# Steps of six score tiles, a fixed accumulator and a factored mixing in a gated-attention and token-mixing kernel

## The chip, the core and the metric

The kernel runs on one core of a Trainium2 chip. The core has five engines with a queue of instructions each: PE (TensorE, matrix products, whose results go to PSUM, eight banks of 512 fp32 columns on 128 partitions), DVE (VectorE), ACT (ScalarE), POOL (GpSimd) and SP, which only issues DMAs here. Each engine works through its queue in order; semaphores hold an instruction until what it reads is there and what it overwrites has been read. The metric is the device time of one execution in microseconds (us).

## The reference

Eight batches, each with a sequence of S = 3200 and a model width of D = 256. z is S x 64, u and v are S x D, and all inputs and the output are fp32.

```python
scores = (1 / S) * z @ z.T                    # S x S per batch
attn   = maximum(scores, 0) ** 2
x      = u * (attn @ v)                       # S x D
wq, wk = x @ w_q, x @ w_k                     # S x 64
W_tok  = (wq @ wk.T) / sqrt(64)               # S x S
out    = maximum(W_tok @ x, 0) @ w_out        # S x D
```

Nothing nonlinear stands between W_tok and x, so the kernel never forms W_tok. It uses W_tok @ x = x @ (w_q @ w_k.T @ G), with G = x.T @ x, a 256 x 256 matrix per batch, and moves all scale factors into one final factor.

## The kernel before, in words

The queries of a batch (columns of the scores) are cut into seven groups of 512, 512, 512, 512, 384, 384 and 384 columns. For each group the kernel goes through 25 tiles of 128 keys. A score tile is a matmul with 64 rows (z has 64 features); zT holds z transposed twice, in partitions 0 to 63 and 64 to 127, so that the two score matmuls of a pair use different halves of the PE array. A pair fills one PSUM tile of two banks (`scores`, L202).

The pair then goes through two stages. `first_stage` writes g = max(4 sc, 0) in fp32 to SBUF, on DVE (L226) or ACT (L222), and so empties PSUM. `second_stage` squares g to fp16, on ACT (L236) or POOL (L238). The result, at, is the stationary side of the second product with v (`outs`, L253), which adds up over the 25 tiles in a tile "acc" of two banks. `gate` multiplies acc by u (L273) and gives x. `turn_x` transposes x by a DMA from SP's queue (L281).

All PSUM tiles (score pairs, acc, and the products named below) take turns in one pool of four slots of two banks.

The work is a software pipeline of steps written out by hand. A step has four score tiles (GRP = 4), and the second product follows three steps later (LAG = 3). In a step, the order on every engine is: scores, first stages, what is due at the start of the step, second stages of the step before, the second product, what is due at the end of the step. `two` puts a product at the end of one step and its eviction at the start of the next.

When a batch's seven groups are done, `gram` makes G (L291), `mixw` multiplies it by M = w_k w_q^T, made once at the start by `weights_1` and `weights_2` (L309, a tile "jtp", in fp32), and then, one group of the following batch at a time, `mix` (L328, four matmuls of the group's width with 128 rows) and `proj` (L350, the product with w_out) make the output, which ACT scales (L387) and SP's queue stores (L388). The last batch's mixing stands at the end by itself, with DVE scaling (L383). xT of a group is thus read a whole batch after it is written.

z of the next batch is loaded in fp32 by SP's queue (L115), cast and transposed in 32 x 32 blocks by DVE in five pieces (`turn_z`, L123 and L124), put in place by eight DMAs (`spread_z`, L131) and doubled by one more (`double_z`, L141). v of the next batch is loaded and cast by a DMA from POOL's queue (`load_v`, L110). z of the first batch is cast and transposed in four pieces, on PE (`transpose_first`, L101).

## Time and profile before

| | |
|---|---|
| median of 3 runs | 953.89 us (953.76 to 954.2) |
| the profiled execution, own time | 955.04 us |
| its span, first to last instruction | 953.2 us |
| PE busy | 919.7 us, 7521 matmuls |
| DVE busy | 702.5 us |
| POOL busy | 611.6 us |
| ACT busy | 544.3 us |
| DMA moved | 92.51 MB, mean 97 GB/s |
| mean granted PE clock | 0.998 of full |

In the views below a line reads: line of the kernel, engine, operation, output <- inputs, shapes, count, then busy time or idle time and what ended it. In a timeline the first column is the start in us from the span's start and the second is how long the run of like instructions took. In a window's row each engine's busy time stands with its count, in the order PE, PEld (weight loads), DVE, ACT, POOL, and then the PE clock, the DMA share and GB/s. In the list of waits the three numbers are total us, times, longest us. A matmul's recorded end is modelled, so PE's busy time covers some short waits. For a DMA, "to landing" is the time from its issue to the last semaphore update.

### The profile page before, as it was taken

Reading aid. Unit: us, or ns where it says so; the run is one execution under the profiler, and the core shown is the slowest. Engines: PE = TensorE matmul, PEld = TensorE weight load, DVE = VectorE, ACT = ScalarE, POOL = GpSimd, SP = SyncE. Lnnn points to the kernel's source line nnn. Section 1 sums busy time; section 2 is a strip of 40 time slices with the busy share of each in tenths; the row PEclk is TensorE's granted clock in tenths of the full one; section 3 lists DMA queues with packets and bytes.
Section 4 is the critical chain, followed back from the end, with each engine's and each line's share of the span. In section 5 each row is a group of like instructions: output and inputs, shape, how many; then the busy total and the mean of one; then the engine's idle time right before and its main releaser. Section 6 shows DMA issues by size and latency. Waiting matters only on the chain.

```text
span 953.2 us, 18224 instructions
## 1 busy us (share of the span) xinstructions
PE 919.7 (96%) x7521; PEld 622.7 (65%) x7521; DVE 702.5 (74%) x760; ACT 544.3 (57%) x627; POOL 611.6 (64%) x375
## 2 busy tenths in 40 slices
PE   6999999999999999999999999999999999999996
PEld 3666676666766666666666667666676666766674
DVE  4988858778587776877678776877758877587753
ACT  4555545566456664566455664655646566466643
POOL 6877756767566764757566665666657666567650
PEclk9999999999999999999999999999999999999999
DMA  9942257432582346632566424843338433123224
GB/s 156 143 82 47 59 90 144 94 93 75 94 157 70 91 104 105 119 90 70 129 80 118 109 77 105 124 94 97 83 88 125 103 88 89 48 74 88 71 71 139
DMA packets 204707, 92.51 MB, mean 97 GB/s; under 512 B 127120, under 2 KB 204176, under 8 KB 204624
## 3 DMA queue, kind: packets, MB, share of 16 engines
q1 hardware_dynamic: 178576, 77.97, 34.2%
q0 software_dynamic: 25776, 13.11, 11.1%
q8 instruction: 59, 0.97, 0.4%
q10 hardware_dynamic: 272, 0.26, 0.1%
q14 instruction: 24, 0.20, 0.1%
HBM read 59.38 MB, written 26.21 MB: 90 GB/s over the span
## 4 chain that ended last, share of the span: by engine, by line
PE 83%; DVE 10%; issue 4%; ACT 2%; DMA 1%; DVEq 0%; ACTq 0%
PE acc L253 51%; PE sc L202 17%; DVE g L226 7%; PE fo L350 5%; PE xtx L291 5%; PE mx L328 4%; PE jtp L309 1%; DVE zs L123 1%; ACT rt L340 1%; DVE x_sb L273 1%; DMA out_dram<-fo 0%; PE ztp L101 0%; ACT g L222 0%; DMA z<-in_z_dram 0%; DVE wo L174 0%
## 5 line engine op out<-in xcount | busy, mean ns | idle before, releaser
L238 POOL TENSOR_TENSOR at<-g 128x1024 f16<-128x1024 f32 (+2 forms) x354 | 595.2, 1694 | 310.5 <-DVE g L226 282.1
L226 DVE TENSOR_SCALAR g<-sc 128x1024 f32<-128x1024 f32 (+2 forms) x562 | 595.2, 1096 | 212.3 <-PE sc L202 201.4
L253 PE MATMUL acc<-v_sb,at 128*128 128x256 f16 x5000 | 608.3, 274 | 0.4 <-DVE g L226 0.4
L253 PEld LDWEIGHTS <-at 128*128 128x128 f16 x5000 | 461.5, 98 | 169.1 <-issue 104.7
L236 ACT ACTIVATE at<-g 128x1024 f16<-128x1024 f32 (+2 forms) x354 | 327.2, 952 | 23.0 <-DVE g L226 21.5
L222 ACT ACTIVATE g<-sc 128x1024 f32<-128x1024 f32 (+2 forms) x146 | 132.8, 913 | 273.5 <-PE sc L202 267.1
L202 PE MATMUL sc<-zT 64*128 64x512 f16 (+1 forms) x1400 | 207.0, 361 | 15.2 <-DVE g L226 11.1
L202 PEld LDWEIGHTS <-zT 64*128 64x128 f16 x1400 | 47.5, 94 | 113.0 <-issue 108.7
L340 ACT ACTIVATE rt<-mx 128x1024 f16<-128x1024 f32 (+1 forms) x56 | 52.0, 931 | 40.1 <-PE mx L328 40.1
L273 DVE TENSOR_TENSOR x_sb<-acc,u_sb 128x512 f16<-128x512 f32 x112 | 65.4, 625 | 9.1 <-PE acc L253 8.8
L350 PE MATMUL fo<-wo,rt 128*128 128x256 f16 x400 | 53.0, 273 | 3.7 <-ACT rt L340 3.7
L387 ACT ACTIVATE fo<-fo 128x1024 f32<-128x1024 f32 (+1 forms) x49 | 45.6, 930 | 17.4 <-PE fo L350 17.4
L328 PE MATMUL mx<-xT_sb,jt 128*128 128x512 f16 (+1 forms) x224 | 52.2, 356 | 0.7 <-ACT jt L320 0.7
L350 PEld LDWEIGHTS <-rt 128*128 128x128 f16 x400 | 38.0, 98 | 12.8 <-ACT rt L340 7.8
L291 PE MATMUL xtx<-x_sb 128*128 128x256 f16 x400 | 45.0, 273 | 0.0
L291 PEld LDWEIGHTS <-x_sb 128*128 128x128 f16 x400 | 39.1, 98 | 4.5
L328 PEld LDWEIGHTS <-jt 128*128 128x128 f16 x224 | 21.6, 98 | 13.4 <-ACT jt L320 1.1
L123 DVE CAST zs<-z 128x320 f16<-128x320 f32 x35 | 24.3, 696 | 0.0
L302 ACT COPY G<-xtx 128x512 f32<-128x512 f32 x8 | 4.7, 584 | 33.7 <-PE xtx L291 33.7
L124 DVE STREAM_TRANSPOSE zst<-zs 128x320 f16<-128x320 f16 x35 | 17.9, 511 | 1.2
L383 DVE TENSOR_SCALAR fo<-fo 128x1024 f32<-128x1024 f32 (+1 forms) x6 | 6.8, 1136 | 14.3 <-PE fo L350 12.3
L309 PE MATMUL jtp<-G,MT 128*128 128x256 f32 x64 | 15.4, 383 | 0.7 <-ACT G L302 0.7
(26 smaller groups left out, 52.1 us busy)
## 6 DMA issues: line engine op xcount, KB each, us to landing
u_sb<-in_u_dram SPq DMA_DIRECT2D x32, 512.0 KB, 5.9
out_dram<-fo SPq DMA_DIRECT2D x32, 512.0 KB, 3.1
v_sb<-in_v_dram POOLq DMA_DIRECT2D x7, 1600.0 KB, 17.8
u_sb<-in_u_dram SPq DMA_DIRECT2D x24, 384.0 KB, 3.6
out_dram<-fo SPq DMA_DIRECT2D x23, 384.0 KB, 2.5
z<-in_z_dram SPq DMA_DIRECT2D x7, 800.0 KB, 6.3
zT<-zst SPq DMA_DIRECT2D x56, 50.0 KB, 2.4
zT<-zT SPq DMA_DIRECT2D x7, 400.0 KB, 4.8
```

Of the source, the lines that this page charges most:

```text
L202: nc.tensor.matmul(out=sc[:, h, 0:gw], lhsT=zT[b][half : half + dqk, ts(ti, P)], rhs=zT[b][half : half + dqk, ds(gs, gw)], start=True, sto ...
L222: nc.scalar.activation(out=g[:, hs, 0:w], in_=sc[:, hs, 0:w], func=RELU, scale=GSCALE)
L226: nc.vector.tensor_scalar(out=g[:, hs, 0:w], in0=sc[:, hs, 0:w], scalar1=0.0, scalar2=GSCALE, op0=AOP.max, op1=AOP.mult,)
L236: nc.scalar.square(out=at[:, hs, 0:w], in_=g[:, hs, 0:w])
L238: nc.gpsimd.tensor_mul(out=at[:, hs, 0:w], in0=g[:, hs, 0:w], in1=g[:, hs, 0:w])
L253: nc.tensor.matmul(out=acc[:, j // 2, ds((j % 2) * D, D)], lhsT=at[:, h, ts(j, P)], rhs=vs[b][:, ti, :], start=(ti == 0 and j % 2 == 0), s ...
L273: nc.vector.tensor_mul(out=xs[b][:, n0 + j : n0 + j + nj, :].rearrange("p n d -> p (n d)"), in0=acc[:, j // 2, 0 : nj * D], in1=u_sb[:, j ...
L291: nc.tensor.matmul(out=ps[:, 0, ds(cc * D, D)], lhsT=xs[b][:, ti, ds(cc * P, P)], rhs=xs[b][:, ti, :], start=(ti == 0 and cc == 0), stop=( ...
L328: nc.tensor.matmul(out=ps[:, db, 0:gw], lhsT=jts[b][:, ac, ds(db * P, P)], rhs=xTs[b][:, gs // P : (gs + gw) // P, ac, :], start=(ac == 0) ...
L340: nc.scalar.activation(out=rt[:, :, 0:gw], in_=ps[:, :, 0:gw], func=RELU)
L350: nc.tensor.matmul(out=ps[:, jf // 2, ds((j - jf) * D, D)], lhsT=rt[:, dc, ts(j, P)], rhs=wo[:, dc, :], start=(dc == 0 and j == jf), stop= ...
L387: nc.scalar.mul(out=flat_out, in_=flat_in, mul=FINAL_SCALE)
```

## The change

- A step has six score tiles (three pairs); a step with a mixing has four. The second product follows at least two steps later (LAG = 2). It takes 25 tiles as 6, 6, 6, 7 or as five times 5, by how far the scores are ahead.
- The accumulator is two tiles of one bank each ("acc0", "acc1"), which every group uses again. The other PSUM tiles share three slots of two banks. In the last step of a group the second product finishes the first bank, then the second, and each is followed by its gate.
- The first stage of one pair goes to ACT unless k is divisible by 3 or the step has a mixing. After a step with a gate, it is ACT that takes the first pair.
- Mixing is factored. `heads` makes w_k^T G (fp32, with w_k doubled so that it fills 128 rows of the result); `queries` makes w_q^T x^T of one group two steps after the group is done, and so reads xT then; `mix` is a pair of 64-row matmuls, ahead of the step's scores, and its eviction comes right after the scores.
- gram, heads, queries and proj are issued after the first ten matmuls of a step's second product, one such product per step, and are evicted in the same step.
- z of the next batch is loaded with a cast by a DMA from POOL's queue, doubled by DVE (`double_z`, 1600 elements) and transposed by one DMA of 25 blocks from SP's queue. The loads of z, v and u fall due by steps counted from a group's first second product.
- At the start, the z pieces are 4, 6, 7 and 8 tiles, cast up front on DVE, ACT and POOL; the weights are only cast, on POOL. At the end, the last batch's mixing runs mix one group ahead of proj.

The core of the diff:

```diff
-    GRP = 4
-    LAG = 3
+    LAG = 2
-    pps = ctx.enter_context(tc.tile_pool(name="pps", bufs=4, space=bass.MemoryType.PSUM))
+    pps = ctx.enter_context(tc.tile_pool(name="pps", bufs=3, space=bass.MemoryType.PSUM))
+    pacc = ctx.enter_context(tc.tile_pool(name="pacc", bufs=1, space=bass.MemoryType.PSUM))
...
+    ZCH = [(0, 4), (4, 6), (10, 7), (17, 8)]
...
     def load_z(b):
+        zds[b] = pz.tile([P, NT, 2, dqk], FP16, tag="zd", name="zd")
+        nc.gpsimd.dma_start(out=zds[b][:, :, 0, :], in_=rows(z, b))
     def double_z(b):
+        nc.vector.tensor_copy(out=zds[b][:, :, 1, :], in_=zds[b][:, :, 0, :])
+    def turn_z(b):
+        zT[b] = pzt.tile([P, S], FP16, tag="zT2", name="zT2")
+        nc.sync.dma_start_transpose(
+            out=zT[b][:].rearrange("p (n s) -> p n s", s=P),
+            in_=zds.pop(b)[:].rearrange("p n a k -> p (n a k)"),
+        )
...
+    def second_product(b, gi, t0, t1):
+        nj = widths[gi] // P
+        last = t1 == NT
+        if t0 == 0:
+            for half in range(2):
+                accs[half] = acc_tile(half, f"acc{half}")
...
+        if last:
+            for half in range(2):
+                for ti in range(t0, t1):
+                    for j in range(2 * half, min(2 * half + 2, nj)):
+                        todo.append(lambda ti=ti, j=j: one(ti, j))
+                run = todo.pop()
+                todo.append(lambda run=run, half=half: (run(), gate(b, gi, half)))
...
+    def queries(b, gi):
+        gw = widths[gi]
+        ps = ps_tile("qq")
         for ac in range(ND):
+            nc.tensor.matmul(
+                out=ps[:, 0, 0:gw],
+                lhsT=wq2[:, ac, :, :].rearrange("p t h -> p (t h)"),
+                rhs=xTs[b, gi][:, 0 : gw // P, ac, :],
+                start=(ac == 0), stop=(ac == ND - 1),
+            )
...
     def mix(b, gi):
         for db in range(ND):
+            half = db * dh
+            nc.tensor.matmul(
+                out=ps[:, db, 0:gw],
+                lhsT=hss[b][half : half + dh, ds(db * P, P)],
+                rhs=qts[b, gi][half : half + dh, 0:gw],
+                start=True, stop=True,
+            )
...
+    def group_done(k, b, gi):
+        if gi == NG - 1:
+            between(k + 1, lambda: gram(b), lambda ps: gram_out(b, ps))
+            between(k + 2, lambda: heads(b), lambda ps: heads_out(b, ps))
+            todo_mix.append((k + 3, b, 0))
+        elif b > 0:
+            todo_mix.append((k + 3, b - 1, gi + 1))
+        between(k + 2, lambda: queries(b, gi), lambda ps: queries_out(b, gi, ps))
+    def group_begun(k, b, gi):
+        if gi + 1 < NG:
+            due(k + 1, lambda: load_u(b, gi + 1))
+        elif b + 1 < B:
+            due(k + 1, lambda: load_u(b + 1, 0))
+        if gi == 0 and b + 1 < B:
+            due(k + 4, lambda: load_z(b + 1))
+            due(k + 5, lambda: load_v(b + 1))
+            due(k + 10, lambda: double_z(b + 1))
+            due(k + 11, lambda: turn_z(b + 1))
...
+        n = 4 if k == 0 else 6
+        if todo_mix and todo_mix[0][0] <= k:
+            _, mb, mg = todo_mix.pop(0)
+            mixing = (mb, mg, mix(mb, mg))
+            n = 4
...
+        act_pair = 0 if (gate_pending or k < 4) else 1
+        for i, (p0, sc) in enumerate(fresh):
+            on_act = i == act_pair and not mixing and (k % 3 != 0 or k < 4 or gate_pending)
+            staged.append((p0, first_stage(p0, sc, on_act)))
+        if len(waiting) == 3:
+            second_on_act = [False, True, k % 2 == 0]
...
+                sizes = [6, 6, 6, 7] if ahead >= 10 or produced == NTILE else [5, 5, 5, 5, 5]
...
+        cut = 10 if extra else 0
+        for fn in matmuls[:cut]:
+            fn()
+        if extra:
+            ps = extra[0]()
+            extra[1](ps)
+        for x in acts[1:]:
+            second_stage(*x)
+        for fn in matmuls[cut:]:
+            fn()
```

## The prediction

> **What bounds the kernel now.** I read the page's shares first, then the windows for start, middle and end, then the timeline of single steps, the list of waits, and last the landing times of the DMAs.

> ```profile
> PE 919.7 (96%) x7521; PEld 622.7 (65%) x7521; DVE 702.5 (74%) x760; ACT 544.3 (57%) x627; POOL 611.6 (64%) x375
> ...
> 0.00:22.00 22.00, 13.21 (x82) 7.21 (x83) 10.01 (x14) 10.45 (x12) 13.27 (x18) 1.00 0.91 148
> 22.00:926.06 904.06, 887.53 (x7306) 601.85 (x7305) 684.23 (x738) 525.62 (x606) 598.36 (x357) 1.00 0.45 94
> 926.06:953.20 27.14, 19.00 (x138) 13.63 (x135) 8.26 (x9) 8.19 (x10) 0.00 (x0) 0.93 0.44 143
> ```

> TensorE (PE) is the bound: in the middle window it lacks 16.5 us of 904. So a change must shorten PE's own work, and any wait that it puts into PE's queue is paid in full. One step of the steady state:

> ```profile
> 410.78 0.60 PE L202 MATMUL sc<-zT 64*128 64x512 f16 x4
> 411.32 1.92 PE L253 MATMUL acc<-v_sb,at 128*128 128x256 f16 x16
> 413.17 0.60 PE L202 MATMUL sc<-zT 64*128 64x512 f16 x4
> ```

> Period 2.39 us. Second-product matmuls start (1.92-0.27)/15 = 0.110 apart; the two score matmuls of a pair run side by side, and pairs 0.60-0.38 = 0.22 apart. 16x0.110 + 2x0.22 = 2.20, so 0.19 per step goes to changing between 64-row and 128-row matmuls and back. Where PE does lose time, scores wait for a PSUM slot that a late VectorE has not emptied:

> ```profile
> 43.80 3.48 DVE L226 TENSOR_SCALAR g<-sc 128x1024 f32<-128x1024 f32 x3
> ...
> 43.85 0.39 PE L202 MATMUL sc<-zT 64*128 64x512 f16 x2
> ...
> 45.07 0.39 PE L202 MATMUL sc<-zT 64*128 64x512 f16 x2 [0.83 <-DVE g L226]
> ...
> PE sc L202 <- DVE g L226: 11.1, 18, 1.1
> PE fo L350 <- ACT rt L340: 3.7, 13, 0.5
> ```

> The second pair came 1.22 after the first where 0.22 was due: 1.0 lost, of which 0.83 shows as idle, because a matmul counts as busy to its modelled end. By start-to-start gaps I find 58 late score pairs and 12 late fo's: 16.5 idle plus 70x0.17 hidden = 28 us.

> Two DMA rows matter later. This is the transpose of x (first the median of all 56, then the one issued at 35.23), and the load of v, issued at 30.98:

> ```profile
> DMA to landing us min/median/max: 2.7/3.1/12.5
> DMA to landing us min/median/max: 11.3/11.3/11.3
> DMA to landing us min/median/max: 16.9/17.8/19.1
> 35.23 1.62 SPq L281 DMA_TRANSPOSE xT_sb<-x_sb  x1
> 30.98 1.59 POOL L110 DMA_DIRECT2D v_sb<-in_v_dram  x1
> ```

> In each of seven batches one x transpose is issued 4 to 7 us after a v load, and these seven land after 10.0 to 12.5 us, the other 49 after 2.7 to 4.9. Today nobody waits for them: xT is read a batch later.

> **The change part by part.** Base: the profiled span, 953.2. Its own time was 955.04, 1.15 above the median 953.89.

> *PE work.* Steps with both products go from 349 to 257 (counted by following the loop): 92x0.19 = -17.6. Mixing had four full matmuls a group, 4x0.217 at 512 and 4x0.161 at 384 columns; now two full ones (queries) and one side-by-side pair. That saves one 0.217/0.161 and some in 49 groups of the loop, 9.3, less 2.4 for six queries of the last batch that come out of the tail into the loop: -6.9. jtp is eight passes of 0.216 a batch, heads four: 7x0.86 = -6.0. The weight product (six matmuls and their fp32 passes) -2.4. Sum -33. The extra products inside the second product add no row change. Nothing covers PE, so this gain is real, if nothing waits.

> *Stalls of before.* All 28 go, since steps, slots and VectorE's z work (35 casts, 35 transposes, 42 us) are gone; what comes instead is counted new.

> *Gates on fixed banks (+29).* The next group's first matmul into each bank now waits for the gate that reads it, and the gate stands on VectorE behind the step's first stages. Groups alternate between steps of 6,6,6,7 and of 5,5,5,5,5; the pair has nine steps, so the last of the fives nearly always has k divisible by 3, where all three first stages are VectorE's. From that step's first score: VectorE begins at 0.50 (scores 406.00, VectorE 406.50), three g take 3.48 (at 43.80), two gates 1.28 (at 408.77) less 0.06 overlap: 5.20. PE begins 20 matmuls at 0.54+0.22 = 0.76, the last at 0.76+19x0.11 = 2.85, the next scores 0.20 later at 3.05, and wants the second bank at 3.05+0.76+0.22 = 4.03. Loss 1.2, 15 times; at 384 columns (three g 2.72 at 915.92, gates 1.02 at 926.26) 1.0, ten times; two longer steps 0.4. After 6,6,6,7 the gate ends at 4.72 and the bank is wanted at 4.91: hidden, by 0.14 after the semaphore. Bounds 0 (VectorE early) and 56x1.2 = 67.

> *Three slots.* Where a queries step has three g on VectorE and a mixing step follows, the third slot is free at 3.98 and its scores are due at 3.70: 0.33, 21 times: +7. Bounds 0 and 28, what slots cost before.

> *ACT.* It gains 56 evictions of queries (0.58 or 0.45 us, 30 us in all); mixing evictions come right after their pair. rt is ready about 0.3 ahead of its projection. +2, bounds 0 and 5 (the 12 late fo's of before).

> *z by DMA.* Gone: on SP 7 loads, 56 spreads (0.65 each) and 7 doublings. New on POOL's queue: a casting load of z, 1.58 like v's, one step before v. POOL has slack (64% busy) and its squares are used two steps later: 0, at most 7x1.6 = 11. New on VectorE: double_z, 1600 elements; the z cast of 320 takes 0.31 to 1.83, 0.70 in the mean, so 1.5 to 9 us, taken as 2. It precedes a step with three g in three batches: 3x1.3 = +4, bounds 0 and 7x3.5 = 25. New on SP: one transpose of 25 blocks, some 25/8x1.25 = 3.9 us of issue with an out DMA behind it; zT is first read at the next batch and the next x transpose is 8 us off: 0, at most 3x0.5.

> *Queries wait for xT (+40).* This is the largest term. turn_x goes out when the second gate ends, queries follow two steps later, after ten matmuls, and PE's queue stands still until xT is there: behind the waiting weight load are the rest of the second product and the next scores, so all engines run dry. From the fives: issue at 5.25, queries at 3.05+3.49+1.2+1.86 = 9.6; from 6,6,6,7: 4.75 and 3.93+3.05+1.86 = 8.84. So xT has 4.1 to 4.35 us; 3.1 is enough, with 1 to spare. But for the first group of batches 0 to 6 the loads of z and v of the next batch are issued in the group's last step or the two after it, and POOL, which runs ahead, issues v 1.5 to 5 us before that turn_x and z some 5 us before v. So these seven transposes meet the loads. Bounds: landing after 3.1, no loss, and after 12.5, 7x8.3 = 58. I take 10.0, the least of the seven rows, as some are issued earlier in v's flight: 7x5.7 = 40.

> [...]

> *Start and end.* Until 22.0 PE has done 9.7 us of work: 12.3 lost. After, the first product waits for POOL's first square, behind five casts (0.44 to 0.60) and three more v issues (0.9), until about 15.7; at 17.4 PE has done 7 and lost 10.4: -2 (bounds -4, +3). In the end phase gram, copy, heads, copy, mixing, projection reach the first output about 1.8 sooner (heads 0.86 for jtp 1.99, mixing pair 0.22 for 0.87), and the last 13 us are the output's in both: -2 (bounds -4, 0).

> Sum: 953.2-33-28-2-2+29+7+2+4+40 = 970.2; plus 1.84 and minus 1.15: median 971.

> **The rivals.**

> *xT is in time (faster).* If the transposes beside the loads land within 4.1 us, the term of 40 is gone: 931. For it: in 49 of 56 rows they do. Against: all seven beside v did not. It decides where 971-954 = 17 of the 40 are gone: 23/7 = 3.3 a wait, so landings under about 7.5 us make the change a gain.

> *Gates cost nothing.* If first stages are done earlier than I step them, 29 goes, but four batches then wait about 1.2 more for xT: 947. Against: 1.28 for two gates and 3.48 for three g are rows.

> *PE comes back slow from its long waits (slower still).* At the start of this trace the first 16 second-product matmuls (13.46) took 3.60 us, later ones 1.92. If each of the seven waits brings that once, 7x1.7 = 12; twice, 24: 983 to 995. In the middle window no idle of PE is longer than 1.1 us, so this trace can't tell.

> [...]

> *It nets out.* Gains of 61 in work and stalls against a loss of the same size, 954: it needs waits for xT of 3.3 us each.

> **How the numbers follow.** Main case, all terms near their size: 0.50, 957 to 985. xT in time: 0.22, 931 (925 to 945). Free gates: 0.08, 947. Slow clock: 0.17, 983 to 995. Even: 0.03. A time within 0.2% (2 us) of 953.9 cannot be told from no change. Faster 0.22 + most of 0.08 = 0.28; same 0.05; slower 0.67. The range must reach into the first rival and most of the third: 935 to 993; the main case alone 957 to 985.

> **What the profile after would show.** PE's second product at 257 stretches of up to 28 matmuls, 0.19 per change. PE (its weight load) waiting on DMA xT some 7 times, 4 to 8 us each, at the first queries of a batch; no other queries late. PE acc waiting on DVE x_sb some 26 times, 1.0 to 1.2. VectorE busy about 670, ACT 580. PE's share falling to about 92%. The prediction is wrong if the seven x transposes land in under 7.5 us, if the loads go out after them, or if a wait that I put at nothing (squares late by two steps, POOL behind its DMA issues) repeats in each group.

## The result: 975.34 us, slower by 2.2%

The changed kernel takes 975.34 us (median of 4 runs, 974.47 to 975.83). The kernel before, run beside it, takes 954.05 (4 runs, 953.76 to 954.87). The ratio is 1.0221, with a 95% interval of 1.0203 to 1.0238. The profiled execution took 975.03, its span 973.3.

The page of the changed kernel, shares of the engines and the granted PE clock in 40 slices:

```profile
PE 899.4 (92%) x7481; PEld 630.8 (65%) x7481; DVE 662.0 (68%) x692; ACT 569.1 (58%) x679; POOL 624.7 (64%) x391
PEclk9899998999989999899999999999999999999999
```

PE has less to do than before (899.4 for 919.7), yet its share fell from 96 to 92%. VectorE, the engine that used to be late, is less busy too. And the clock row has dips that come about once a batch. The windows say where the idle time lies (columns as for the kernel before):

```profile
0.00:18.00 18.00, 11.75 (x61) 5.42 (x63) 8.25 (x10) 8.10 (x9) 12.95 (x19) 1.00 1.11 208
18.00:935.00 917.00, 857.56 (x7176) 603.44 (x7173) 639.02 (x665) 543.74 (x647) 605.41 (x369) 0.98 0.45 89
947.00:973.30 26.30, 18.14 (x145) 13.02 (x142) 8.17 (x9) 8.41 (x11) 0.00 (x0) 0.94 0.48 148
```

Start and end are a little shorter than before. In the middle PE lacks 59 us of 917; before it lacked 16.5 of 904. The list of waits of the changed kernel (total us, times, longest) names what PE lacked:

```profile
PE qq L302 <- DMA xT_sb<-x_sb: 38.8, 10, 6.5
PE sc L167 <- DVE g L190: 11.1, 27, 0.7
PE acc L219 <- DVE x_sb L245: 9.1, 41, 0.3
PE fo L343 <- ACT rt L333: 1.1, 2, 0.9
```

Two thirds of it are the queries, which wait for the transposed x. Six of the ten waits there, one in each of batches 0, 1, 2, 3, 5 and 6, are 5.2 to 6.5 us long and make 35.7 of the 38.8. This is the one of batch 1, in the timeline of the changed kernel, with the load of v ahead of it, and then the landing of all 56 x transposes:

```profile
141.89 1.58 POOL L116 DMA_DIRECT2D v_sb<-in_v_dram  x1
...
146.81 1.31 SPq L257 DMA_TRANSPOSE xT_sb<-x_sb  x1
...
150.08 1.26 PE L219 MATMUL acc<-v_sb,at 128*128 128x256 f16 x10
...
156.51 1.04 PE L302 MATMUL qq<-xT_sb,wq 128*128 128x512 f16 x2 [5.17 <-DMA xT_sb<-x_sb]
...
157.34 3.19 PE L219 MATMUL acc<-v_sb,at 128*128 128x256 f16 x14
```

```profile
DMA to landing us min/median/max: 2.7/3.1/10.7
```

SP issues the transpose at 146.81. PE does its ten matmuls, wants xT at 151.3 and gets it at 156.5. The last line of the timeline shows the second cost: fourteen second-product matmuls take 3.19 us, 0.22 apart instead of 0.11. The windows around that wait of the changed kernel show the granted clock (the seventh figure after the stretch, ahead of the DMA share):

```profile
151.30:154.60 3.30, 0.05 (x1) 0.00 (x0) 0.89 (x1) 0.70 (x1) 3.30 (x2) 1.00 1.35 179
154.60:161.40 6.80, 4.89 (x22) 2.53 (x22) 0.00 (x0) 1.83 (x3) 0.28 (x1) 0.50 0.49 103
161.40:168.20 6.80, 6.80 (x62) 5.22 (x59) 4.77 (x5) 4.68 (x5) 3.00 (x2) 1.00 0.23 77
```

3.3 us into the wait the clock drops to one half, and it stays there for 6.8 us, of which 4.9 are work after the wait. Each of the six long waits has one such stretch.

To compare kernels I added up, over the middle of each, how much later each PE matmul started than the one before it made due. Due is the pace seen where nothing waits: 0.109 us for 256 columns, 0.096 and 0.093 for a change from 128 to 64 rows and back, and a 64-row pair side by side. These sums also hold what a matmul's modelled end hides, and are estimates, good to some 2 us; the two late output products of the list lie in the end phase, outside the stretch.

| us | before | after |
|---|---|---|
| stretch summed | 22 to 926 | 18 to 947 |
| work of PE, at due pace | 871.5 | 841.6 |
| queries wait for xT | 0 | 41.6 |
| half clock, on top of the waits | 0 | 11.7 |
| scores wait for a slot | 21.7 | 18.6 |
| second product waits for a bank (a gate) | 0.9 | 15.7 |
| output product waits for rt | 5.1 | 0 |
| pace and small rests | 4.8 | -0.3 |
| lost, in all | 32.5 | 87.3 |

Work fell by 29.9 and losses rose by 54.8, so the middle grew by 24.9. Start and end gave back 4.8 (22.0 to 18.0, and 27.1 to 26.3). That is 20.1, the difference of the spans.

### The profile page after: what moved, and what is told of

Same layout as the page of the kernel before. It is cut to its first block, busy times and chain, and to the rows that moved or that the text cites. A ratio compares the mean times of both kernels' runs of the same rounds, so it can differ in the third digit from the quotient of the medians.

```text
span 973.3 us, 17971 instructions
## 1 busy us (share of the span) xinstructions
PE 899.4 (92%) x7481; PEld 630.8 (65%) x7481; DVE 662.0 (68%) x692; ACT 569.1 (58%) x679; POOL 624.7 (64%) x391
## 4 chain that ended last, share of the span: by engine, by line
PE 76%; DMA 10%; DVE 10%; issue 3%; POOL 1%; ACT 1%; DVEq 0%; SPq 0%; ACTq 0%
PE acc L219 49%; PE sc L167 13%; DMA xT_sb<-x_sb 9%; DVE g L190 7%; PE xtx L269 4%; PE fo L343 4%; DVE x_sb L245 3%; PE qq L302 2%; PE mx L321 2%; PE hd L285 1%; DMA z<-in_z_dram 1%; DMA out_dram<-fo 0%; ACT at L200 0%; POOL v_sb L92 0%; POOL zd L103 0%
## 5 line engine op out<-in xcount | busy, mean ns | idle before, releaser
L202 POOL TENSOR_TENSOR at<-g 128x1024 f16<-128x1024 f32 (+3 forms) x357 | 594.9, 1682 | 314.7 <-DVE g L190 283.0
L219 PE MATMUL acc<-v_sb,at 128*128 128x256 f16 x5000 | 622.4, 276 | 9.5 <-DVE x_sb L245 9.1
L219 PEld LDWEIGHTS <-at 128*128 128x128 f16 x5000 | 475.4, 99 | 166.5 <-issue 87.1
L200 ACT ACTIVATE at<-g 128x1024 f16<-128x1024 f32 (+1 forms) x351 | 325.9, 957 | 0.0
L167 PE MATMUL sc<-zT 64*128 64x512 f16 (+1 forms) x1400 | 189.3, 362 | 13.7 <-DVE g L190 11.1
L167 PEld LDWEIGHTS <-zT 64*128 64x128 f16 x1400 | 58.2, 95 | 94.2 <-issue 67.0
L314 ACT CAST qt<-qq 128x512 f16<-128x512 f32 (+1 forms) x56 | 30.2, 539 | 78.2 <-PE qq L302 77.9
L302 PE MATMUL qq<-xT_sb,wq 128*128 128x512 f16 (+1 forms) x112 | 33.4, 382 | 39.1 <-DMA xT_sb<-x_sb 38.8
L367 ACT ACTIVATE fo<-fo 128x1024 f32<-128x1024 f32 (+2 forms) x50 | 46.3, 926 | 31.6 <-PE fo L343 30.5
L321 PE MATMUL mx<-qt,hs 64*128 64x512 f16 (+1 forms) x112 | 21.0, 375 | 0.3 <-ACT rt L333 0.2
```

Source lines behind the costliest of these rows:

```text
L167: nc.tensor.matmul(out=sc[:, h, 0:gw], lhsT=zT[b][half : half + dqk, ts(ti, P)], rhs=zT[b][half : half + dqk, ds(gs, gw)], start=True, sto ...
L200: nc.scalar.square(out=at[:, hs, 0:w], in_=g[:, hs, 0:w])
L202: nc.gpsimd.tensor_mul(out=at[:, hs, 0:w], in0=g[:, hs, 0:w], in1=g[:, hs, 0:w])
L219: nc.tensor.matmul(out=accs[j // 2][:, ds((j % 2) * D, D)], lhsT=at[:, h, ts(j, P)], rhs=vs[b][:, ti, :], start=(ti == 0 and j % 2 == 0), ...
L302: nc.tensor.matmul(out=ps[:, 0, 0:gw], lhsT=wq2[:, ac, :, :].rearrange("p t h -> p (t h)"), rhs=xTs[b, gi][:, 0 : gw // P, ac, :], start=( ...
L367: nc.scalar.mul(out=flat_out[:, sl], in_=flat_in[:, sl], mul=FINAL_SCALE)
```

## The experiments

Each is one edit to the changed kernel, unless more is said. Sums of losses are made as in the table above. In the texts of what was expected, runs are numbered in the order in which they were made: the first and second have the queries at k + 4 and k + 3, the third the shifted remainder, the fourth v in pieces, and the eighth k + 3 with the fourth step.

### What the waits for xT cost

The first moves the queries two steps later (k is the step in which a group ends).

```diff
-        between(k + 2, lambda: queries(b, gi), lambda ps: queries_out(b, gi, ps))
+        between(k + 4, lambda: queries(b, gi), lambda ps: queries_out(b, gi, ps))
```

> The queries of a group are due four steps after the group's end, not two. My theory: PE stands still for xT because the x transpose shares the DMA engines with the load of v, and then runs at half clock for a while. Two more steps (6 to 8 us) cover the 10 us of the landing, so the 42 us of waits and some 13 us at half pace go: 920 us, no PE wait on xT over 1 us, no half clock before the end phase. Rival (the waits only show a lateness that POOL, VectorE or the DMA queue would bring anyway): PE waits as long at another place, over 955 us.

Measured: 931.20 (930.62 to 931.67, 4 runs), 0.9759 of before (0.9742 to 0.9775). The landing of its x transposes, and two lines of its list of waits:

```profile
DMA to landing us min/median/max: 2.7/3.1/11.1
```

```profile
PE sc L167 <- DVE g L190: 19.4, 46, 0.7
...
PE qq L302 <- DMA xT_sb<-x_sb: 0.4, 1, 0.4
```

The transposes land as late as before the edit (six after 9.6 to 11.1 us), but nobody stands waiting, and the half clock is gone up to the end phase. Time fell by 44 us. The losses show 53 gone (41.6 of waits, 11.7 of clock) and 8 come in their place: waits for slots and banks grew from 34.3 to 41.9.

The second moves them one step.

```diff
-        between(k + 2, lambda: queries(b, gi), lambda ps: queries_out(b, gi, ps))
+        between(k + 3, lambda: queries(b, gi), lambda ps: queries_out(b, gi, ps))
```

> The queries are due three steps after the group's end. The six waits of 5 to 6.7 us shrink by one step, some 3.5 us, to 2 to 3 us each. [...]

Measured: 937.18 (one run). I had put it at 975 - 25 - 13 = 937 if the half clock (13) went with 25 of the waits, and at 950 if it stayed. The number is the first of these, but not for a reason that I had given. k + 3 is a mixing step from batch 1 on, where no other product may go, so there the queries went to k + 4. One long wait was left, in batch 0:

```profile
PE qq L302 <- DMA xT_sb<-x_sb: 4.4, 1, 4.4
```

It brought one stretch of half clock, again 6.8 us long. So this run doesn't weigh waits against clock as it was meant to. It shows one stretch of half clock with the one wait that was left.

### Which load holds the transposes up

Here v of the next batch comes in three pieces, each issued three steps after a group's end, when that group's transpose has long been issued. z stays where it was.

```diff
+    VCH = [(0, 9), (9, 8), (17, 8)]
-    def load_v(b):
-        vs[b] = pv.tile([P, NT, D], FP16, tag="v_sb", name="v_sb")
-        nc.gpsimd.dma_start(out=vs[b][:], in_=rows(v, b))
+    def load_v(b, c):
+        if c == 0:
+            vs[b] = pv.tile([P, NT, D], FP16, tag="v_sb", name="v_sb")
+        n0, nn = VCH[c]
+        nc.gpsimd.dma_start(out=vs[b][:, n0 : n0 + nn, :], in_=rows(v, b)[:, n0 : n0 + nn, :])
...
+        if gi < 3 and b + 1 < B:
+            due(k + 3, lambda: load_v(b + 1, gi))
...
-            due(k + 5, lambda: load_v(b + 1))
```

> The queries stay two steps after the group's end; the load of v is cut in three pieces (9, 8 and 8 tiles), each due three steps after the end of one of the batch's first three groups, so that no x transpose is under way with one. The load of z stays where it is. If the load of v is what delays xT: all x transposes land within about 5 us, waits and half clock go, 920 us as with later queries. If the load of z or the transposes of z do it: still 10 us, 970 us or more.

Measured: 927.07 (one run; before beside it 954.42). The landing of its x transposes:

```profile
DMA to landing us min/median/max: 2.7/3.1/4.7
```

All 56 land within 4.7 us. The waits for xT are 4.2 in all, in eleven small pieces, and no half clock is left up to the end phase. So it is the load of v. That z, in the last 1.7 us of its flight, does no harm shows in the changed kernel itself, in batch 4, whose transpose went out with z under way and 0.44 us ahead of v. From its timeline:

```profile
503.90 1.58 POOL L120 DMA_DIRECT2D zd<-in_z_dram  x1
...
509.40 1.24 SPq L257 DMA_TRANSPOSE xT_sb<-x_sb  x1
509.84 1.59 POOL L116 DMA_DIRECT2D v_sb<-in_v_dram  x1
...
513.36 0.21 PEld L302 LDWEIGHTS <-wq 128*128 128x128 f16 x2
```

z lands 7.2 us after its issue, so it was still moving; the transpose landed after 3.1, and the queries came at 513.4 without a long wait. In batch 2 the order was the other way round, v at 265.06 and the transpose at 266.46, and that one took 10.7. In the run with pieces no transpose goes out while a piece is on its way, so it is the order that helped there; whether a smaller piece would hold a transpose up as well, no run shows.

### Gates and slots

This shifts by one step the steps whose three first stages are all VectorE's, so that they no longer fall on the last step of a group of fives (the shifted remainder: k divided by 3 leaves 1, not 0).

```diff
-            on_act = i == act_pair and not mixing and (k % 3 != 0 or k < 4 or gate_pending)
+            on_act = i == act_pair and not mixing and (k % 3 != 1 or k < 4 or gate_pending)
```

> Only the remainder of k that gives VectorE all three first stages is changed, from 0 to 1, so that the last step of five fives has two on VectorE and one on ACT. My theory of the gate (VectorE's queue ahead of the gate, not the fixed banks themselves): the 34 us of waits for slots and banks fall to about 10 (the last step of 6,6,6,7 now has three, 0.3 each), while the waits for xT grow by 1.2 in three or four batches: 955 us. Rival (one set of accumulator banks costs the wait by itself): 970 to 975 us, and PE still waits some 25 times for x_sb after the fives.

Measured: 956.62 (953.84 to 957.18, 10 runs), 1.0018 of before (1.0009 to 1.0028). Its list of waits:

```profile
PE qq L302 <- DMA xT_sb<-x_sb: 39.9, 10, 7.1
...
PE acc L219 <- DVE x_sb L245: 2.6, 14, 0.2
PE sc L167 <- DVE g L190: 2.5, 7, 0.5
```

Losses at banks and slots fell from 34.3 to 14.8, while the waits for xT (43.5) and the clock (11.0) stayed. So the two groups of losses are separate, and 19.5 of the 34.3 came from where the modulo put VectorE's heavy steps. Such a step, from the timeline of the changed kernel:

```profile
240.25 3.49 DVE L190 TENSOR_SCALAR g<-sc 128x1024 f32<-128x1024 f32 x3
240.83 1.47 PE L219 MATMUL acc<-v_sb,at 128*128 128x256 f16 x12
...
242.24 0.81 PE L167 MATMUL sc<-zT 64*128 64x512 f16 x4
...
243.65 1.01 DVE L245 TENSOR_TENSOR x_sb<-acc,u_sb 128x512 f16<-128x512 f32 x2
243.79 0.39 PE L167 MATMUL sc<-zT 64*128 64x512 f16 x2 [0.74 <-DVE g L190]
244.38 1.36 PE L219 MATMUL acc<-v_sb,at 128*128 128x256 f16 x10 [0.21 <-DVE x_sb L245]
```

The third g ends at 243.74. PE's third score pair needs that slot and comes at 243.79, 1.11 after its due time (242.24 + 2x0.22). Only then does PE reach the bank, 0.28 late. One late VectorE costs 1.4, most of it at the slot.

### What the half clock costs

Here forty matmuls of 256 columns, whose results nothing uses, stand ahead of the queries of group 0 in batches 0 to 6. They add work, but PE is then not idle while it waits.

```diff
     def queries(b, gi):
...
+        if gi == 0 and b + 1 < B:
+            for _ in range(40):
+                nc.tensor.matmul(
+                    out=ps[:, 0, 0:D],
+                    lhsT=wq2[:, 0, :, :].rearrange("p t h -> p (t h)"),
+                    rhs=vs[b][:, 0, :],
+                    start=True,
+                    stop=True,
+                )
```

> The changed kernel with 40 additional matmuls of 256 columns (4.4 us, results never used) ahead of the queries of the first group of batches 0 to 6, where PE waits for xT. They fill most of each wait, so that PE is idle for some 2 us and not 5 to 6.7. If the half clock after the waits costs 13 us on top of the waits: it is gone, the batch that had no wait pays 4.4 us, 966 us. If the half clock only fell into time that was lost anyway: 975 to 980 us.

Measured: 968.76 (967.34 to 970.94, 4 runs), 1.016 of before (1.0142 to 1.0178). It is 6.6 us faster than the changed kernel, with 30.5 us more work. The same wait as above, in its timeline:

```profile
152.38 4.53 PE L303 MATMUL qq<-v_sb,wq 128*128 128x256 f16 x40
157.89 0.59 PE L311 MATMUL qq<-xT_sb,wq 128*128 128x512 f16 x2 [0.98 <-DMA xT_sb<-x_sb]
158.32 1.69 PE L219 MATMUL acc<-v_sb,at 128*128 128x256 f16 x14
```

The fourteen matmuls after the wait take 1.69 us where they took 3.19. In all, the extra work and the waits left over (14.2) make 44.7 for 41.6, slightly more, because batch 4 now pays as well; the loss to the clock went from 11.7 to 2.8. So the half clock is a cost of its own on top of the waiting: 8.9 of its 11.7 us went while PE lost no less to waits and added work.

### How far the repairs add up

The load of v in pieces and the shifted remainder together:

> v in three pieces as in the fourth run and the remainder 1 as in the third. If the two causes are independent, the fourth run's 927 loses what the third took off the waits for slots and banks, 34 to 15 us: 908 us. If the waits for slots and banks were only low in the third run because PE was resting for xT, 920 us or more.

Measured: 908.30 (907.67 to 909.66, 4 runs), 0.9524 of before (0.951 to 0.9539). They add: the losses left are slots 7.1, banks 9.0 and xT 3.9.

The load of v in pieces, and all three first stages on VectorE only in the fourth step of a group taken as five fives, when the second product has reached its tile 15:

```diff
-            on_act = i == act_pair and not mixing and (k % 3 != 0 or k < 4 or gate_pending)
+            on_act = i == act_pair and not mixing and (k < 7 or tiles[consumed][2] != 15)
```

> v in three pieces; VectorE has all three first stages only in the fourth step of a group taken as five fives, which holds neither a gate nor another product. Theory of the gate: waits of PE for slots and banks fall under 10 us, 900 to 905 us. Rival: ACT, with some 25 more first stages of 1 us, becomes late with its squares or with rt and PE waits for it: 910 us or more.

Measured: 910.48 (909.07 to 911.41, 4 runs), 0.9548 (0.9533 to 0.9564); my expectation was too low. The banks cost 0.4 now, but 15.6 of waits for slots stayed, 3.5 of them in batch 0 behind a slow `double_z` (below). The rival's number came without its cause: PE's scores wait 21 times for VectorE's g, by its list of waits, and never for ACT. In the fourth step, three g take VectorE 3.48 us, and PE's own work on five tiles takes 3.05 by the prediction's figures, so at 512 columns the next step's third pair comes 0.55 late (at 168.19, for instance). In the run with k + 3 below, the queries stand in that very step and give PE 0.43 more to do, and the pair is only 0.12 late. So VectorE's heavy work cost less here in the step that held another product (0.12) than in the one that held none (0.55).

The queries at k + 4 with the shifted remainder:

> Queries four steps after the group's end and the remainder 1. In the first run the waits for slots rose to 27 us, from 19, though nothing of VectorE's work was moved. If they are VectorE's three first stages in a step that also has the queries, this run has few of them: 905 to 910 us. If later queries cost slots by themselves: 915 us or more.

Measured: 901.46 (one run; before beside it 953.83), with slots 5.8 and banks 4.4. That is below what I had expected; later queries do not cost slots by themselves. The queries at k + 3, v in one piece, and the fourth step of the fives:

> Queries three steps after the group's end and three first stages for VectorE only in the fourth of five fives; the load of v in one piece. The second run left one wait for xT, in the first batch. 937 less the 33 us that the gate theory takes off 42: about 905 us.

Measured: 899.48 (one run). Banks 0.4, slots 6.1; one wait for xT is left, in batch 0, 3.6 us long, with one stretch of half clock, 3.4 us long. So the last run takes that one away too, with the queries of batch 0 at k + 4:

```diff
-        between(k + 2, lambda: queries(b, gi), lambda ps: queries_out(b, gi, ps))
+        between(k + (4 if b == 0 else 3), lambda: queries(b, gi), lambda ps: queries_out(b, gi, ps))
...
-            on_act = i == act_pair and not mixing and (k % 3 != 0 or k < 4 or gate_pending)
+            on_act = i == act_pair and not mixing and (k < 7 or tiles[consumed][2] != 15)
```

> The eighth run with the queries of batch 0 one step later still, which takes away its last wait for xT (3.8 us with 1.3 us at half pace after it): 895 us. Rival: another wait takes its place in batch 0, 899 us.

Measured: 900.02 (899.13 to 900.60, 4 runs), 0.9435 of before (0.9421 to 0.9449). It beats both kernels, but it missed my expectation of 895, and the rival's 899 came true: it gained nothing over the run before it (899.48). The two differ in batch 0 alone, since from batch 1 on k + 3 is a mixing step and the queries stand at k + 4 in both. The page of this kernel, and what happens in batch 0, from its timeline:

```profile
PE 877.3 (98%) x7481; PEld 623.7 (70%) x7481; DVE 637.2 (71%) x661; ACT 598.5 (67%) x710; POOL 623.3 (69%) x391
```

```profile
43.74 7.44 POOL L202 TENSOR_TENSOR at<-g 128x1024 f16<-128x1024 f32 x4
...
47.27 4.36 DVE L123 COPY zd<-zd 128x1600 f16<-128x1600 f16 x1
...
49.90 0.39 PE L167 MATMUL sc<-zT 64*128 64x512 f16 x2
51.55 4.59 DVE L190 TENSOR_SCALAR g<-sc 128x1024 f32<-128x1024 f32 x4
...
52.80 0.39 PE L167 MATMUL sc<-zT 64*128 64x512 f16 x2 [2.51 <-DVE g L190]
```

Without the wait for xT, POOL squares without a gap, until 51.18. `double_z`, which takes 0.58 us where POOL is idle, ends 0.45 after that, at 51.63, and the scores wait 2.5 for a slot; a stretch of half clock (3.4 us) follows. One wait has taken the place of another, at the same price: 11.0 us are lost in the middle, and 10.8 in the kernel with that wait for xT.

The shortest of these runs (899.5 to 901.5, two of them single runs, too near each other to rank) are bound by PE again: 98% busy in the last, with some 11 us lost in the middle. The work of PE is the same at 975 and at 900; what differs is the step in which the queries stand and the step in which VectorE takes all three first stages.

## Why the prediction was right, point by point

The forecast was 971, in a range of 935 to 993 and with slower as the likely sign; the time is 975.3. The terms of the span, beside what the trace shows:

| term, us | predicted | measured |
|---|---|---|
| work of PE, start and end | -33 -2 -2 | -34.7 (-29.9 -4.8) |
| stalls of before that go | -28 | -32.5 |
| queries wait for xT | +40 | +41.6 |
| gates on fixed banks | +29 | +15.7 |
| three slots | +7 | +18.6 |
| ACT, `double_z`, small rests | +6 | about 0 |
| half clock | 0, a rival's | +11.7 |
| span | 970.2 | 973.3 |

**Work of PE.** Right in size. PE's own work did fall, and nothing covered it.

**xT.** The largest term was right in its place, its cause and its size: the transposes behind v's load landed after 9.7 to 10.7 us (predicted 10.0), while the other fifty took 2.7 to 5.1. It was six waits of about 6 rather than seven of 5.7, since in batch 4 the transpose slipped out ahead of v. The rival that has xT in time (931) fell, and the run in which it is in time gave 927. It was sound to go by the rows of the trace before (10.0 to 12.5 beside v), and not by their median of 3.1.

**Gates and slots.** The sum was right, 34.3 for 36, the split was not. The step that failed is the one that lets PE reach the second bank at 4.03 after three g that end at 3.98: by its own numbers the third score pair was due at 3.49 and needed the slot that the third g frees at 3.98. PE so loses the time at the slot first, and comes to the bank when its gate is nearly done. The profile said so at once: not 26 bank waits of 1.0 to 1.2, but 41 of at most 0.3, and 27 at slots.

**Half clock.** I left this out of the sum, as a rival of 12 to 24 us with a chance of 0.17. It happened, in every long wait, at 11.7, just under that rival's lower end. So the main case and this rival came true together, and that the sum still came within 3 us of the span is in part luck: other terms had put the time too high, the stalls of before by 4.5 (the table's 4.8 of small rests, which I had not counted), ACT and `double_z` by 6, gates and slots by 2. The trace before could not tell, since no idle time of PE in its middle was longer than 1.1 us. With the landing that I had taken, 10.0, I had put the waits at 5.7 myself; in the runs 5.2 to 6.5 us brought the half clock each time, and less would have done (last section).

**What the profile was to show.** VectorE at 662 (about 670 predicted), ACT at 569 (580) and PE at 92% came as foreseen. Four short waits for xT, 3.1 us in all, came where no other queries were to be late.

## What to carry to other kernels

When a product is moved closer to the transfer that feeds it, look for the same transfer beside the heaviest load of the trace and take that row, not the median: here the median was 3.1 us and the row that counted was 10. Where PE's queue stood still for 2.2 us or longer, the clock here was at half for 3.4 or 6.8 us (after one wait of 2.24 it was not), so count the work after such a wait as slower too. A helper's late step was paid mostly at the first thing of it that PE needed (1.11 us at the slot, 0.28 at the bank), so walk through the waits in the order in which PE meets them, and then move the late step, which here was one number in a modulo. Put it where PE has other work: three first stages on VectorE cost 0.12 us in the step that held the queries and 0.55 in the same step without them.

## What the runs showed of the hardware

**The clock's stretches lie on a grid.** In the changed kernel they start at 42.0, 154.6, 274.1, 397.0, 629.1, 752.0 and 970.4. All the distances are whole multiples of 3.413 us: 33, 35, 36, 68, 36 and 64 of them. Waits of 4.4 us and longer brought 6.8 us at half clock, waits of 2.2 to 3.6 us brought 3.4, and shorter ones (up to 1.5) none. But of two waits of the same length, 2.22 us in the run with k + 4 and the shifted remainder and 2.24 in that with v in pieces and the shifted remainder, the first brought such a stretch and the second did not.

What tells them apart is how much of the idle time falls into one window of the grid. Take the traces of all twelve kernels in windows of 3.413 us, from each one's first change of clock (at 16 to 20 us) to its end. At full clock, 31 windows have PE idle by its records for 1.91 us or more, and the clock drops at the end of every one; in the other 3126 PE is idle for 1.89 us or less, and it drops after none. At half clock, it comes back after all 19 windows with 0.46 us of idle time or less and stays for another after all 18 with 1.08 or more. Each of the two waits has a second one of 0.74 us behind it, and the grid parts the idle time into 1.06 and 1.91 us in the first run and into 1.33 and 1.65 in the second.

**The copy of z on VectorE ends 0.45 us after a squaring of POOL.** In the eleven profiles from the changed kernel on there are 77 `double_z`. Eight found POOL idle (two of them 0.04 us after they began) and took 0.58 us. The other 69 each ended 0.445 to 0.454 us after a squaring of POOL had ended. Two of them, from the changed kernel and then from the last run:

```profile
52.23 5.59 POOL L202 TENSOR_TENSOR at<-g 128x1024 f16<-128x1024 f32 x3 [2.11 <-DVE g L190]
57.44 0.83 DVE L123 COPY zd<-zd 128x1600 f16<-128x1600 f16 x1
```

```profile
262.14 5.59 POOL L202 TENSOR_TENSOR at<-g 128x1024 f16<-128x1024 f32 x3 [1.58 <-DVE g L190]
...
266.57 1.62 DVE L123 COPY zd<-zd 128x1600 f16<-128x1600 f16 x1
```

POOL ends at 57.82 and the copy at 58.27; POOL ends at 267.73 and the copy at 268.19. In four of the 77 it had to outwait two or three squarings in a row and took 4.1 to 4.4 us. So the time of such a copy was not its own 0.58 here: it was set by what was left of the squaring in flight, and in those four cases by the next ones too. Why they let more than one squaring pass, no run tells. And POOL pays as well: in 17 cases its next squaring followed at once, the copy came in between, and that squaring took 2.20 to 2.21 us, where 1.89 is the median.

**A transpose behind v's load.** In the changed kernel the DMA transpose issued 1.4 us after the load of v (batch 2) took 10.7 us to land and the one issued 0.44 us before it (batch 4) took 3.1, though they come from different queues (SP's and POOL's). The late one did not wait until v was in: it landed at 277.2, and v at 282.8. What in the load held it up, no run here tells.
